# Block attention and a Fourier-mixing MLP on one core: the down product of the last batch in seven block products

## The chip, the cores and the metric

One core of a Trainium2 chip runs the whole program. The metric is device time in microseconds (us) for one execution. The engines are TensorE (PE; the loads of its stationary operand are shown as PEld), VectorE (DVE), ScalarE (ACT), GpSimd (POOL) and SyncE (SP), which issues most transfers.

## The reference

Inputs are q, k, v of shape 4 x 8 x 768 x 64 (batch, heads, positions, width) and two weight matrices, 512 x 2048 and 2048 x 512, all f32. Cut to what matters:

```python
# attention: each position sees its own block of 64 and the best 3 blocks by q . mean(k), causally
attn = softmax(where(mask, q @ k.T / 8, -1e9)) @ v
x    = attn as 4 x 768 x 512                      # heads side by side
u    = x + real(fft(fft(x, axis=1), axis=2))      # Fourier mixing
un   = (u - mean(u)) / sqrt(var(u) + 1e-6)        # over the last axis
out  = u + relu(un @ w_ch1) @ w_ch2               # the MLP: up, relu, down
```

## The kernel before, in words

The kernel works in stages that overlap. `attention(p)` treats a pair of heads, 16 pairs in all, four to a batch: casts (line 688) and small differences (461, 466) on POOL or DVE, transposes on TensorE (478, 527), block means and gates (497, 514, 542), the choice of three blocks on DVE (561 to 585), a POOL memset for a position's own block (594), the mask's transpose (606) and its spelling into extra rows of the query tile (616), scores (639), exponentials on ACT (650), the causal corners on POOL (656), and the product with v (668, `attend`), scaled on DVE (677, 680). `fourier(b)` mixes a batch: folds of x on DVE or POOL (700, 711, 721), two stages of products (739, 743; 773), the residual (779), statistics (786, 789), normalisation (813, 817) and a transpose into `unT` (831, 688).

`mlp(b)` works on a batch of 768 rows in two halves of 384. In a half the up product makes 16 tiles, each 128 hidden units by 384 rows, from four steps of 384 columns (line 853). Relu (865 on ACT, 867 on DVE) writes them as f16 into `hT[half]`. The down product makes three row tiles of 128 x 512, each from 16 steps of 512 columns over the hidden units (line 878); the stationary operand is a 128 x 128 piece of `hT`, the moving one a tile of `w2`. DVE adds the result to `U`, which holds u, in place (line 884), and SyncE writes the 128 x 512 tile out (256 KB; the call at 887, issued by the helper at 367).

No order is written by hand. `Plan.op` collects every operation with what it reads and writes, a rank, and an assumed duration for each engine that could do it. `Plan.schedule` then lays all operations out in time by those durations: on each engine it takes the operation that can start first, ties by rank, and where two engines could do a thing, it chooses the one that would end it earlier. The eight PSUM banks are handed out there as well, with a cap for each kind. The order found is what the engines execute. A POOL operation marked `port` waits for the DVE operation marked `port` ahead of it. Products of an earlier batch's MLP so fill TensorE while attention waits for other engines; the last batch's MLP, number 3, has nothing left beside it.

Of the kernel before, what the change touches and what calls it, by code (L numbers as in the profile page):

```python
# [12 lines left out]
FP = mybir.dt.float32  # L13
F16 = mybir.dt.float16
# [4 lines left out]
OP = mybir.AluOpType  # L19

S = 768
DM = 512
NB = 12
NST = 6
# [58 lines left out]
class Plan:  # L83
# [53 lines left out]
    def schedule(self):  # L137
        ops = self.ops
        free = dict(PE=1.0, ACT=1.5, DVE=0.9, POOL=0.9, SP=0.75)
        ready = {e: [] for e in free}  # L140
        for o in ops:
            o.wait = len(o.deps)
            o.ready = o.rel
            for d in o.deps:
                ops[d].users.append(o.i)
        cand = {e: set() for e in free}

        def offer(o):
# [12 lines left out]
        order = []  # L161
        left = len(ops)
        while left:
            best = None
            for e, c in cand.items():
                now = free[e]
                pick = None
                for i in c:
                    o = ops[i]
                    t = o.ready  # L170
                    blocked = False
                    for p in o.ps:
                        if p.bank is None:
                            if used[p.kind] >= self.CAPS[p.kind] or not banks:
                                blocked = True
                                break
                            t = max(t, banks[0][0])
                    if blocked:
                        continue
                    if o.port and e in ("DVE", "POOL"):  # L180
                        t = max(t, port_free + (self.LAT["DVE"] if e == "POOL" and holder else 0.0))
                    if o.dma and e != "POOL" and len(landing[e]) >= self.DEPTH:
                        t = max(t, landing[e][-self.DEPTH])
                    if len(o.engs) > 1:
# [36 lines left out]
            if o.dma:  # L221
                mine, other = ("POOL", "SP") if e == "POOL" else ("SP", "POOL")
                go = max(dma_free[mine], free[e])
                shared = max(0.0, dma_free[other] - go)
                dma_free[mine] = go + (2 * o.dma if 2 * o.dma <= shared else o.dma + shared / 2)
                o.done = dma_free[mine] + 1.9
                landing[e].append(o.done)
            order.append(o)
            left -= 1
            for p in o.ps:  # L230
                p.left -= 1
                if p.left == 0:
                    heapq.heappush(releases, (o.done, p.bank, p.kind))
            for u in o.users:
                v = ops[u]
                v.wait -= 1
                at = o.done
                if e in v.engs and len(v.engs) == 1 and not o.dma:
                    at = free[e] + self.OWN[e]
                elif o.dma:  # L240
                    at += self.LANDING if st > 8.0 else 0.0
                elif "PE" in v.engs and o.done > self.SLACK_FROM:
                    at += self.SLACK
                v.ready = max(v.ready, at)
# [29 lines left out]
PT_W = _w  # L274
# [4 lines left out]
def kernel(  # L279
# [9 lines left out]
    nc = tc.nc  # L289
    B, H, _, D = q.shape  # L290
# [30 lines left out]
    w2 = sb([128, NIT, DM], F16, "w2")  # L321
    eps = sb([128, 1], FP, "eps")

    NQ, NH, NG, NV, NPT = 2, 2, 2, 3, 2
    qn = many(NQ, [128, 2, NST, 64], FP, "qn")
    kn = many(NQ, [128, NST, 2, 64], FP, "kn")
    vn = many(2, [128, 2, NST, 64], FP, "vn")
    qhl = many(NH, [128, 2, NST, 128], F16, "qhl")
    k16 = many(NH, [128, NST, 128], F16, "k16")
    klo = many(1, [128, NST, 128], F16, "klo")  # L330
    QG = [many(NG, [128, S], F16, f"qg{e}") for e in range(2)]
    ki_all = sb([128, 2 * NG, S], F16, "ki")
    KI = [[ki_all[:, 2 * i + e, :] for i in range(NG)] for e in range(2)]
    V16 = many(NV, [128, 2, NST, 66], F16, "v16")
# [10 lines left out]
    pm = sb([128, 2, 6, 257], F16, "pm")  # L345
# [17 lines left out]
    P = Plan()  # L363


    def dma(rank, e, dst, src, w, us, r=(), issue=0.45, rel=0.0):
        P.op(rank, {e: issue if e != "POOL" else 0.65}, lambda x, n: eng[x].dma_start(dst, src),
             r=r, w=w, dma=us, rel=rel)
# [5 lines left out]
    def small(rank, e, cost, fn, r=(), w=(), ps=(), pre=(), port=False, rel=0.0):  # L374
        engs = e if isinstance(e, dict) else {e: cost}
        P.op(rank, engs, fn, r=r, w=w, ps=ps, pre=pre, port=port, rel=rel)
# [464 lines left out]
            P.readers.setdefault(("x", x3, 0), []).append(P.last_w[("unT", st)])  # L841


    def mlp(b):
        base = 100000 + 1000 * b
        U, u2 = ub[b % 2], b % 2
        for hf in range(2):
            for it in range(NIT):
                hp_ = P.psum("mm")
# [12 lines left out]
                def relu(x, n, hf=hf, it=it, hp_=hp_):  # L862
# [3 lines left out]
                    else:  # L866
# [85 lines left out]
```

## Time and profile before

| | us |
|---|---|
| median of 3 runs (lowest, highest) | 313.94 (313.51, 314.13) |
| the profiled execution | 313.72 |
| its span, first to last instruction | 311.5 |
| TensorE busy | 301.3 |
| VectorE busy | 195.3 |
| ScalarE busy | 189.1 |
| GpSimd busy | 130.3 |

The granted TensorE clock is 0.999 of full speed over the span. How to read the rows: in the page's engine rows each digit is the busy share of one of 40 equal slices, in tenths. A row of a group has line, engine, operation, output and inputs with their shapes, a count, then the busy time in us, the mean duration of one in ns, and the engine's idle time ahead of them with what ended it. A row in order of time begins with its start and its length in us; rows that follow each other are merged (x3). Durations of neighbours on an engine can overlap, since they are pipelined. A row of a stretch (two times joined by a colon) has the length, the busy time and count of PE, PEld, DVE, ACT and POOL, the granted clock, the busy share of the DMA engines and the GB/s that they moved.

### The profile page before, as it was taken

What the parts mean: (1) busy time and instruction counts of PE and PEld (TensorE: products, weight loads), DVE (VectorE), ACT (ScalarE), POOL (GpSimd) and SP (SyncE); (2) the same over time, 40 slices, a digit from 0 to 9 for tenths busy, and PEclk for the clock granted to TensorE, in tenths of its full rate; (3) what the DMA queues carried; (4) which work ended last, traced back from release to release, by engine and by line L of the source; (5) the groups of instructions that cost most, each with busy time, mean ns of one, the idle gap of its engine ahead of it and who ended that gap; (6) DMA issues with size and microseconds to landing.
All of it is one profiled execution on the core that took longest, in us unless ns stands there. A gap on an engine that the chain in (4) does not pass through costs nothing.

```text
span 311.5 us, 8060 instructions
## 1 busy us (share of the span) xinstructions
PE 301.3 (97%) x3097; PEld 198.5 (64%) x3097; DVE 195.3 (63%) x652; ACT 189.1 (61%) x418; POOL 130.3 (42%) x251
## 2 busy tenths in 40 slices
PE   7999999999999999999999999999999999999994
PEld 4767676766647776666666876757655865554641
DVE  4797989997655899755548797856425694002001
ACT  2579898779508788478644699708661671540710
POOL 4258897836546181748273453837025000000000
PEclk9999999999999999999999999999999999999999
DMA  8999999990066351009320760010001001101001
GB/s 218 257 241 238 246 232 217 228 189 22 0 153 176 81 121 32 36 37 237 78 61 34 187 154 1 36 36 35 2 36 67 2 1 67 37 0 67 36 34 67
DMA packets 82085, 31.12 MB, mean 100 GB/s; under 512 B 75272, under 2 KB 77492, under 8 KB 82048
## 3 DMA queue, kind: packets, MB, share of 16 engines
q1 hardware_dynamic: 77584, 25.77, 33.7%
q0 software_dynamic: 3536, 4.56, 8.1%
q8 instruction: 24, 0.39, 0.5%
q10 hardware_dynamic: 928, 0.30, 0.4%
q14 instruction: 13, 0.11, 0.1%
HBM read 28.52 MB, written 6.29 MB: 112 GB/s over the span
## 4 chain that ended last, share of the span: by engine, by line
PE 80%; DVE 9%; ACT 6%; issue 1%; DMA 1%; SPq 0%; DVEq 0%; ACTq 0%
PE bank L878 27%; PE bank L853 26%; PE bank L639 9%; PE bank L668 5%; ACT pt L650 4%; PE bank L527 3%; PE bank L739 2%; DVE u L779 2%; PE bank L773 2%; PE bank L478 2%; PE bank L831 1%; DMA kn<-in_k_dram 1%; DVE bst L786 1%; DVE qg L616 1%; PE bank L492 1%
## 5 line engine op out<-in xcount | busy, mean ns | idle before, releaser
L650 ACT ACTIVATE pt<-bank 128x512 f16<-128x512 f32 x192 | 88.3, 579 | 23.4 <-PE bank L639 21.7
L853 PE MATMUL bank<-unT,w 128*128 128x384 f16 x512 | 90.7, 326 | 0.2 <-DVE unT L688 0.2
L878 PE MATMUL bank<-w,hT 128*128 128x512 f16 x384 | 89.1, 379 | 0.0
L865 ACT ACTIVATE hT<-bank 128x384 f16<-128x384 f32 x115 | 56.3, 497 | 46.4 <-PE bank L853 45.6
L853 PEld LDWEIGHTS <-w 128*128 128x128 f16 x512 | 48.2, 98 | 30.0 <-issue 0.8
L878 PEld LDWEIGHTS <-hT 128*128 128x128 f16 x384 | 36.0, 98 | 37.6
L639 PE MATMUL bank<-qg,ki 76*128 76x128 f16 (+3 forms) x384 | 51.2, 259 | 0.7 <-ACT pt L650 0.4
L884 DVE TENSOR_TENSOR u<-bank,u 128x512 f32<-128x512 f32 x24 | 16.5, 688 | 51.1 <-PE bank L878 51.0
L639 PEld LDWEIGHTS <-ki 76*128 76x128 f16 x384 | 29.2, 97 | 10.6 <-issue 0.6
L656 POOL TENSOR_SCALAR_AFFINE_SELECT pt<-pt 128x512 f16<-128x512 f16 (+1 forms) x44 | 22.0, 522 | 25.3 <-ACT pt L650 20.6
L668 PEld LDWEIGHTS <-pt 128*128 128x128 f16 x672 | 23.8, 97 | 6.5 <-ACT pt L650 3.0
L668 PE MATMUL bank<-v,pt 128*128 128x65 f16 x672 | 25.6, 193 | 0.6 <-ACT pt L650 0.3
L616 DVE TENSOR_SCALAR qg<-bank 12x384 f16<-12x384 f16 x64 | 20.6, 322 | 7.6 <-PE bank L606 5.7
L466 POOL TENSOR_TENSOR klo<-kn,k 128x384 f16<-128x384 f32 x24 | 21.9, 913 | 5.3 <-DVE rcp L677 1.9
L461 POOL TENSOR_TENSOR qhl<-qn,qhl 128x320 f16<-128x320 f32 x26 | 20.6, 792 | 6.2 <-DVE qhl L688 4.8
L688 POOL CAST k<-kn 128x384 f16<-128x384 f32 x24 | 12.2, 507 | 19.2 <-DVE fs L721 9.0
L688 DVE COPY ki<-bank 64x768 f16<-64x768 f16 x23 | 12.7, 554 | 9.6 <-PE bank L478 7.0
L680 DVE TENSOR_TENSOR x<-bank,rcp 128x384 f16<-128x384 f32 x32 | 17.8, 555 | 0.6
L677 DVE RECIPROCAL rcp<-bank 128x6 f32<-128x6 f32 x32 | 6.2, 193 | 18.0 <-PE bank L668 10.6
L527 PE MATMUL bank<-sm,qhl 128*128 128x128 f16 x192 | 17.1, 229 | 0.1
L779 DVE TENSOR_TENSOR u<-bank,x 128x512 f32<-128x512 f32 x24 | 15.3, 681 | 1.9 <-PE bank L773 1.9
L594 POOL MEMSET gmp<- 64x5 f16 x40 | 4.6, 114 | 27.9 <-DVE gmp L585 26.8
(106 smaller groups left out, 405.6 us busy)
## 6 DMA issues: line engine op xcount, KB each, us to landing
out_dram<-u SPq DMA_DIRECT2D x24, 256.0 KB, 2.0
kn<-in_k_dram SPq DMA_DIRECT2D x28, 192.0 KB, 3.4
vn<-in_v_dram SPq DMA_DIRECT2D x28, 192.0 KB, 3.8
qn<-in_q_dram SPq DMA_DIRECT2D x26, 192.0 KB, 4.4
w<-in_moe_w_ch_dram POOLq DMA_DIRECT2D x16, 256.0 KB, 6.7
hT<-in_k_dram SPq DMA_DIRECT2D x4, 192.0 KB, 4.3
hT<-in_q_dram SPq DMA_DIRECT2D x4, 192.0 KB, 4.2
hT<-in_v_dram SPq DMA_DIRECT2D x4, 192.0 KB, 3.7
```

Source lines behind the costliest of these rows:

```text
L466: lambda x, n, kh=kh, kl=kl, e=e: eng[x].tensor_tensor(out=kl, in0=kn[a][:, :, e, :], in1=kh, op=OP.subtract),
L527: nc.tensor.transpose(bank16[tq.bank][:, 128 * st:128 * st + 128], qhl[h2][:, e, st, :], id16)
L616: nc.vector.tensor_scalar(out=rows[:, i::2, :], in0=turned[at:at + NB, 0:3 - i, :], scalar1=-NEG, scalar2=NEG, op0=OP.mult, op1=OP.add)
L639: nc.tensor.matmul(bank32[sp.bank][:, co:co + a1 - a0], KI[e][g3][0:76, 128 * jt:128 * jt + 128], QG[e][g3][0:76, a0:a1], start=not added, ...
L650: lambda x, n, sp=sp, pt=pt, at=at, wid=wid: nc.scalar.activation(out=pt[:, at:at + wid], in_=bank32[sp.bank][:, 0:wid], func=AF.Exp, scal ...
L656: lambda x, n, pt=pt, at=at, nd=nd: nc.gpsimd.affine_select(out=pt[:, at:at + 128 * nd].rearrange("p (a c) -> p a c", a=nd), in_=pt[:, at: ...
L668: nc.tensor.matmul(o[:, st, 0:65], pt[:, col:col + 128], V16[v4][:, e, jt, 0:65], start=(i == 0), stop=(i == 20))
L688: return eng[x].tensor_copy(out=dst, in_=src)
L779: lambda x, n, kt=kt, mp=mp: nc.vector.tensor_tensor(out=U[:, kt, :].rearrange("p (l r) -> p r l", r=2), in0=bank32[mp.bank].rearrange("p ...
L853: nc.tensor.matmul(bank32[hp_.bank][:, 0:384], w1[:, dt, 128 * it:128 * it + 128], unT[:, dt, 384 * hf:384 * hf + 384], start=(dt == 0), s ...
L865: nc.scalar.activation(out=o, in_=i_, func=AF.Relu)
L878: nc.tensor.matmul(bank32[cp.bank], hT[hf][:, it, 128 * j:128 * j + 128], w2[:, it, :], start=(it == 0), stop=(it == NIT - 1))
```

## The change

The last batch's down product is a 768 x 2048 by 2048 x 512 product. It is cut into 2 x 2 blocks on each side: rows into the two halves, hidden units into two times eight tiles, output columns into two times 256. Eight block products become seven by the scheme of Strassen: five sums of blocks on each side, seven products, and twelve additions or subtractions of their results into the four quarters of the output.

- `weight_sums` makes the five sums of quarters of `w2` on DVE, each in two instructions of 128 x 1024, into `WB`.
- `hidden_sums` makes the five sums of quarters of the hidden activations on DVE, tile by tile of 128 x 384, as soon as relu has written the tiles: 40 instructions, into `HA`.
- `down_seven` runs, for each of three pairs of row tiles, seven products of eight steps with 256 columns, and adds each into one or two quarters of `U` on DVE, 128 x 256 at a time. A quarter that is complete is written out at once (128 KB): twelve transfers.
- `WB` and `HA` need space. The buffers of attention are cut from four larger tiles (`loads_`, `turned_`, `keys_`, `vals_`), and `WB` and `HA` lie over parts of two of them; they wait for the last readers of what they cover.
- In the planner the test for a free bank is written for several new banks at once.

For the last batch both halves of the up product come first and the down product then. The other batches are computed as before.

```diff
--- Plan.schedule
-                    blocked = False
-                    for p in o.ps:
-                        if p.bank is None:
-                            if used[p.kind] >= self.CAPS[p.kind] or not banks:
-                                blocked = True
-                                break
-                            t = max(t, banks[0][0])
-                    if blocked:
-                        continue
+                    new = [p for p in o.ps if p.bank is None]
+                    if new:
+                        if len(banks) < len(new) or any(
+                                used[p.kind] + len(new) > self.CAPS[p.kind] for p in new):
+                            continue
+                        t = max(t, banks[len(new) - 1][0])
--- buffers
-    qn = many(NQ, [128, 2, NST, 64], FP, "qn")
-    kn = many(NQ, [128, NST, 2, 64], FP, "kn")
...
-    PT = [many(NPT, [128, PT_W], F16, f"pt{e}") for e in range(2)]
+    loads_ = sb([128, 11520], F16, "loads")
+    turned_ = sb([128, 16896], F16, "turned")
...
+    qn = [cut(loads_, 4608 * i, 1536, 2, NST, dtype=FP) for i in range(NQ)]
...
+    PT = [[cut(turned_, PT_W * (2 * i + e), PT_W) for i in range(NPT)] for e in range(2)]
...
+    WB = [cut(loads_, 2048 * i, 2048, 8) for i in range(5)]
+    HA = [cut(turned_, 3072 * i, 3072, 8) for i in range(5)]
--- new, before mlp
+    SUMS = [(0, 3, OP.add), (2, 3, OP.add), (0, 1, OP.add), (2, 0, OP.subtract),
+            (1, 3, OP.subtract)]
+    OTHER = [(0, 3, OP.add), (1, 3, OP.subtract), (2, 0, OP.subtract), (0, 1, OP.add),
+             (2, 3, OP.add)]
+    def combine(rank, name, at, dst, x0, x1, op, r, n, pre):
+        small(rank, {"DVE": 0.05 + 0.00059 * n, "POOL": 0.12 + 0.00195 * n}, 0,
+              lambda x, n_: eng[x].tensor_tensor(out=dst, in0=x0, in1=x1, op=op),
+              r=r, w=[(name,) + at], pre=pre, port=True)
+    def weight_sums(rank):
+        for i, (a0, a1, op) in enumerate(OTHER):
+            for c in range(2):
+                src = quarter(lambda kh, nh: w2[:, 8 * kh + 4 * c:8 * kh + 4 * c + 4,
+                                                256 * nh:256 * nh + 256])
+                combine(rank, "WB", (i, c), WB[i][:, 4 * c:4 * c + 4, :], src[a0], src[a1], op,
+                        [("w2", g) for g in range(8)], 1024, UNDER["WB"]())
+    GOES = {1: [(0, OP.add), (3, OP.add)], 2: [(2, OP.add), (3, OP.subtract)],
+            3: [(1, OP.add), (3, OP.add)], 4: [(2, OP.add), (0, OP.add)],
+            5: [(1, OP.add), (0, OP.subtract)], 6: [(3, OP.add)], 7: [(0, OP.add)]}
+    DONE = {3: 1, 4: 2, 7: 0, 6: 3}
+    def hidden_sums(rank, g):
+        for i, (a0, a1, op) in enumerate(SUMS):
+            src = quarter(lambda mh, kh: hT[mh][:, 8 * kh + g, :])
+            keys = quarter(lambda mh, kh: ("hT", mh, 8 * kh + g))
+            combine(rank, "HA", (i, g), HA[i][:, g, :], src[a0], src[a1], op,
+                    [keys[a0], keys[a1]], 384, UNDER["HA"]())
+    def down_seven(b):
+        for j in range(3):
+            cols = slice(128 * j, 128 * j + 128)
+            A = {3: hT[0][:, 0:8, cols], 4: hT[1][:, 8:16, cols]}
+            A.update({i: HA[z][:, :, cols] for i, z in IDX.items()})
+            Bm = {2: w2[:, 0:8, 0:256], 5: w2[:, 8:16, 256:512]}
+            Bm.update({i: WB[z] for i, z in JDX.items()})
...
+            for i in (5, 2, 1, 4, 3, 7, 6):
+                mp = P.psum("mm")
+                def prod(x, n, i=i, mp=mp, A=A, Bm=Bm):
+                    for z in range(8):
+                        nc.tensor.matmul(bank32[mp.bank][:, 0:256], A[i][:, z, :], Bm[i][:, z, :],
+                                         start=(z == 0), stop=(z == 7))
+                P.op(base + 150 + j, {"PE": 0.86}, prod, r=need[i], w=[mp], ps=[mp])
+                for q_, sign in GOES[i]:
+                    small(base - 200000, "DVE", 0.33,
+                          lambda x, n, mp=mp, q_=q_, sign=sign, part=part: nc.vector.tensor_tensor(
+                              out=part(q_), in0=part(q_), in1=bank32[mp.bank][:, 0:256], op=sign),
+                          r=[mp, key(q_)] + pre_u, w=[key(q_)], ps=[mp])
+                    if i in (3, 4, 7, 6) and q_ == DONE[i]:
+                        dma(base - 200000, "SP",
+                            out[b, 128 * row:128 * row + 128, 256 * half:256 * half + 256],
+                            part(q_), [("out", b, row, half)], 0.5, r=[key(q_)])
--- mlp
+        seven = b == B - 1
+        if seven:
+            weight_sums(102160)
...
+                if seven and hf and it >= 8:
+                    hidden_sums(base - 200000, it - 8)
+            if seven:
+                continue
...
+        if seven:
+            down_seven(b)
```

More of the change, by code (lines that the diff above doesn't have):

```diff
@@ L324, with cut @@
     NQ, NH, NG, NV, NPT = 2, 2, 2, 3, 2
-    qn = many(NQ, [128, 2, NST, 64], FP, "qn")
-    kn = many(NQ, [128, NST, 2, 64], FP, "kn")
[L327 to L332, printed above, removed]
+    loads_ = sb([128, 11520], F16, "loads")
+    turned_ = sb([128, 16896], F16, "turned")
+    keys_ = sb([128, 3072], F16, "keys")
+    vals_ = sb([128, 2376], F16, "vals")
+    def cut(t, at, n, *dims, dtype=F16):
+        v_ = t[:, at:at + n]
+        v_ = v_ if dtype == F16 else v_.bitcast(dtype)
+        names = "abc"[:len(dims)]
+        return v_ if not dims else v_.rearrange(
+            f"p ({' '.join(names)} z) -> p {' '.join(names)} z", **dict(zip(names, dims)))
+    qn = [cut(loads_, 4608 * i, 1536, 2, NST, dtype=FP) for i in range(NQ)]
+    kn = [cut(loads_, 4608 * i + 1536, 1536, NST, 2, dtype=FP) for i in range(NQ)]
+    vn = [cut(loads_, 4608 * i + 3072, 1536, 2, NST, dtype=FP) for i in range(2)]
+    klo = [cut(loads_, 9216, 768, NST)]
+    k16 = [cut(loads_, 9984 + 768 * i, 768, NST) for i in range(NH)]
+    qhl = [cut(turned_, 10752 + 1536 * i, 1536, 2, NST) for i in range(NH)]
+    QG = [[cut(turned_, 13824 + 1536 * i + 768 * e, 768) for i in range(NG)] for e in range(2)]
+    ki_all = cut(keys_, 0, 3072, 2 * NG)
     KI = [[ki_all[:, 2 * i + e, :] for i in range(NG)] for e in range(2)]
-    V16 = many(NV, [128, 2, NST, 66], F16, "v16")
+    V16 = [cut(vals_, 792 * i, 792, 2, NST) for i in range(NV)]
     GA = many(2, [128, 24], F16, "ka")
@@ L344 @@
     fs = sb([128, 2, 3, DM], F16, "fs")
-    pm = sb([128, 2, 6, 257], F16, "pm")
+    pmf = sb([128, 3084], F16, "pm")
+    pm = pmf.rearrange("p (r t d) -> p r t d", r=2, t=6)
     fk = fs.rearrange("p r t d -> p (r t) d").rearrange("p t (i d) -> p t i d", i=4)
@@ L841, in fourier, with below @@
             P.readers.setdefault(("x", x3, 0), []).append(P.last_w[("unT", st)])
+    def below(*names):
+        return [k_ for k_ in list(P.last_w) if isinstance(k_, tuple) and k_[0] in names]
+    UNDER = dict(
+        WB=lambda: below("qn", "kn", "vn", "klo", "k16"),
+        HA=lambda: below("pt", "qg", "qm", "qh", "ql", "qz"),
+    )
+    SUMS = [(0, 3, OP.add), (2, 3, OP.add), (0, 1, OP.add), (2, 0, OP.subtract),
+            (1, 3, OP.subtract)]
+    OTHER = [(0, 3, OP.add), (1, 3, OP.subtract), (2, 0, OP.subtract), (0, 1, OP.add),
+             (2, 3, OP.add)]
@@ new lines, in combine, with quarter @@
+    def combine(rank, name, at, dst, x0, x1, op, r, n, pre):
+        small(rank, {"DVE": 0.05 + 0.00059 * n, "POOL": 0.12 + 0.00195 * n}, 0,
+              lambda x, n_: eng[x].tensor_tensor(out=dst, in0=x0, in1=x1, op=op),
+              r=r, w=[(name,) + at], pre=pre, port=True)
+    def quarter(get):
+        return [get(0, 0), get(0, 1), get(1, 0), get(1, 1)]
+    def weight_sums(rank):
[5 more added lines that the diff above has]
+                        [("w2", g) for g in range(8)], 1024, UNDER["WB"]())
@@ new lines, in down_seven @@
+    def down_seven(b):
+        base = 100000 + 1000 * b
+        U, u2 = ub[b % 2], b % 2
+        for j in range(3):
[4 more added lines that the diff above has]
+            Bm.update({i: WB[z] for i, z in JDX.items()})
+            need = {i: ([("HA", IDX[i], g) for g in range(8)] if i in IDX else
+                        [("hT", int(i == 4), (8 if i == 4 else 0) + g) for g in range(8)])
+                    + ([("WB", JDX[i], z) for z in range(2)] if i in JDX else
+                       [("w2", (0 if i == 2 else 4) + z) for z in range(4)]) for i in range(1, 8)}
+            place = [(j, 0), (j, 1), (3 + j, 0), (3 + j, 1)]
+            part = lambda q_, place=place: U[:, place[q_][0], 256 * place[q_][1]:256 * place[q_][1] + 256]
+            key = lambda q_, place=place: ("u", u2, place[q_][0], place[q_][1])
+            pre_u = [("u", u2, st) for st in (j, 3 + j)]
+            for i in (5, 2, 1, 4, 3, 7, 6):
[6 more added lines that the diff above has]
+                for q_, sign in GOES[i]:
+                    row, half = place[q_]
+                    small(base - 200000, "DVE", 0.33,
[6 more added lines that the diff above has]
+                            part(q_), [("out", b, row, half)], 0.5, r=[key(q_)])
```

2 lines of the change are left out of this document (added).

## The prediction

> **What bounds the kernel now.** I read the page first, then the chain of work that ended last, then the rows of the stages that the change touches.
>
> ```profile
> span 311.5 us, 8060 instructions
> PE 301.3 (97%) x3097; PEld 198.5 (64%) x3097; DVE 195.3 (63%) x652; ACT 189.1 (61%) x418; POOL 130.3 (42%) x251
> ...
> PE   7999999999999999999999999999999999999994
> ...
> DVE  4797989997655899755548797856425694002001
> ...
> POOL 4258897836546181748273453837025000000000
> ```
>
> TensorE (PE) is busy for 97% of the span, in nearly every slice at 9, so what counts is TensorE's own time. VectorE (DVE) has room, most of all in the last quarter. GpSimd (POOL) has nothing from slice 32 on. The chain, in order of time (start, length, what):
>
> ```profile
> 247.03 2.62 PE bank L773 x24
> ...
> 261.80 4.10 PE bank L878 x19
> 265.90 10.40 PE bank L853 x64
> 276.31 10.36 PE bank L878 x48
> 286.67 10.40 PE bank L853 x64
> 297.06 10.37 PE bank L878 x48
> 307.44 0.04 DVEq L884
> 307.47 0.04 issue
> 307.52 0.69 DVE u L884
> ```
>
> From 265.90 to 307.43 only the last batch's MLP runs: up product (L853), down product (L878), each in two halves, gapless on TensorE, and then one addition (L884) and the output. The profiled execution took 313.72 us for its span of 311.5; the median of the runs is 313.94, 0.22 above it. I sum against 313.72 and add the 0.22.
>
> **TensorE in the down product.** Before: 96 steps of 512 columns in 10.36 + 10.37 = 20.73 us, 215.9 ns each. After: 7 products x 3 row pairs x 8 = 168 steps of 256 columns, each with its own weight load. Such steps stand in the trace: L773, 24 steps of 256 columns, a new weight load at each, 2.62 / 24 = 109.2 ns. 168 x 109.2 = 18.35 us. **Term 1: -2.38 us.**
>
> The row to doubt is the weight load, since there are 72 more of them:
>
> ```profile
> L878 PEld LDWEIGHTS <-hT 128*128 128x128 f16 x384 | 36.0, 98 | 37.6
> L668 PE MATMUL bank<-v,pt 128*128 128x65 f16 x672 | 25.6, 193 | 0.6 <-ACT pt L650 0.3
> ```
>
> A load is busy 98 ns, under 109.2; and L668, with a load at each step and only 65 columns, has 38 ns per step (25.6 / 672), so loads overlap each other and hide. The Trainium skill, "TensorE: Matmul & The Clock Gate", section "Back-to-back issue gap", speaks against the change: it gives a sustained stream of load and matmul 131 ns per step at 512 columns and about 81 at 128, which by a straight line between them is 98 ns at 256; by it 96 steps would be 12.6 us and 168 steps 16.4, a loss of 3.8 us. The trace does not bear the page out: 215.9 and 109.2 ns here.
>
> **VectorE's sums of hidden activations** (`hidden_sums`, 40 of 128x384, all f16 in SBUF). Rows by shape, and three neighbours in the order of time:
>
> ```profile
> L680 DVE TENSOR_TENSOR x<-bank,rcp 128x384 f16<-128x384 f32 x32 | 17.8, 555 | 0.6
> L884 DVE TENSOR_TENSOR u<-bank,u 128x512 f32<-128x512 f32 x24 | 16.5, 688 | 51.1 <-PE bank L878 51.0
> L700 DVE TENSOR_TENSOR fs<-x 128x384 f16<-128x384 f16 x25 | 8.0, 352 | 0.2
> ...
> 235.30 0.36 DVE L700 TENSOR_TENSOR fs<-x 128x384 f16<-128x384 f16 x1
> 235.57 0.68 DVE L884 TENSOR_TENSOR u<-bank,u 128x512 f32<-128x512 f32 x1
> ```
>
> The two rows with f32 input from PSUM give 1.04 ns per column and 0.155 us fixed. The f16 row of 384 takes 0.352, so 0.51 ns per column, and the next instruction starts 0.27 after it: unwaited instructions overlap by 0.08. In the changed kernel's instruction order, 16 of the 40 sums need activations of the first 24 tiles and lie under the second up product, where VectorE is idle (the zeros in its row). The last 24 come as triplets, one per tile of the last eight. When those tiles come:
>
> ```profile
> 295.80 0.49 ACT L865 ACTIVATE hT<-bank 128x384 f16<-128x384 f32 x1 [0.16 <-PE bank L853]
> 296.45 0.49 ACT L865 ACTIVATE hT<-bank 128x384 f16<-128x384 f32 x1 [0.16 <-PE bank L853]
> 297.10 0.49 ACT L865 ACTIVATE hT<-bank 128x384 f16<-128x384 f32 x1 [0.16 <-PE bank L853]
> ```
>
> One each 0.65 us, the last ending 0.53 after its product's stage (297.59 against 297.06). After the change the second up product follows the first at once: from 276.31 to 286.71. The ninth tile is ready at 286.71 + 0.53 - 7 x 0.65 = 282.69, and eight triplets of 3 x 0.27 = 0.81 end at 289.2 (not overlapping, at 0.352: 291.1). TensorE starts the products in the order 5, 3, 4, 6, 2, 1, 7 for the first row pair; 5, 3, 4 and 6 need nothing of the triplets. At 8 x 109.2 = 0.874 each it comes to product 2 at 290.21 and to its last step at 290.97. So the sums are in time by 1.8 us, and at the slower reading about level. Cost 0; the cover is those four products, and without it up to 0.2 us.
>
> **VectorE's additions into the result** (36 of 128x256 instead of 6 of 128x512, in `down_seven`). By the two f32 rows one is 0.155 + 256 x 0.00104 = 0.42 us, 0.34 overlapped. Twelve per row pair are 4.1 us beside 6.1 us of products. They queue behind the triplets: start 289.2, first row pair at product speed from 291 on. Eight banks hold the products meanwhile: the ninth, at 286.71 + 8 x 0.874 = 293.7, needs the bank of the first, which is added by 290. Cost 0. Their own reads after writes lie two or more instructions apart, which lets them overlap; if none overlapped, see the rivals. At the very end one addition of 256 columns stands where one of 512 stood: 0.69 to 0.42, **term 2: -0.27 us.**
>
> **The output in quarters.** 12 transfers of 128 KB for 6 of 256 KB: each still 128 rows, of 1 KB instead of 2.
>
> ```profile
> 308.24 0.33 SPq L367 DMA_DIRECT2D out_dram<-u  x1
> out_dram<-u SPq DMA_DIRECT2D x24, 256.0 KB, 2.0
> 301.00:304.50 3.50, 3.50 (x18) 1.61 (x17) 0.73 (x2) 0.00 (x0) 0.00 (x0) 1.00 0.20 75
> 308.00:311.50 3.50, 0.00 (x0) 0.00 (x0) 0.21 (x1) 0.00 (x0) 0.00 (x0) 0.88 0.20 75
> ```
>
> An issue takes SyncE 0.33 us and lands 2.0 later; the last four come 0.87 apart or a little less, so the queue keeps up. In a stretch of 3.5 us with one transfer the engines are busy for 0.20 x 3.5 = 0.70 us. Halving the bytes saves between 0 (fixed cost per piece) and 0.35 (all by bytes); nearer to bytes than to pieces is unknown, I take 0.25. **Term 3: -0.25 us.** The Trainium skill, "DMA: Bandwidth & Descriptors", section "Anatomy of one DMA", has 2.0 us fixed plus bytes at 436 GB/s (fitted to another queue kind), which would make it 0.30; the 2.0 us to landing here already contains the transfer.
>
> **VectorE's sums of weights** (`weight_sums`, 10 of 128x1024). By the f16 row: 0.155 + 1024 x 0.00051 = 0.68 us, 0.60 overlapped, 6 us in all, among the last pair's attention. The planner also moves work there: one up product ahead of L514 (`spread`), the second L668 (`attend`) behind the gates (L542) and three more up products, L606 (`m_turn`) behind four down steps.
>
> ```profile
> 216.97 0.20 PE L514 MATMUL bank<-ka,sm 128*128 128x24 f16 x2
> ...
> 218.97 0.80 PE L668 MATMUL bank<-v,pt 128*128 128x65 f16 x21
> 219.61 0.40 PE L542 MATMUL bank<-kg,qg 128*128 128x24 f16 x10
> ...
> 226.30 1.04 PE L639 MATMUL bank<-qg,ki 76*128 76x128 f16 x9
> ...
> 216.97 0.20 DVE L677 RECIPROCAL rcp<-bank 128x6 f32<-128x6 f32 x1 [0.84 <-ACT pt L650]
> 217.20 0.56 DVE L680 TENSOR_TENSOR x<-bank,rcp 128x384 f16<-128x384 f32 x1
> ...
> 221.50 0.81 DVE L581 MAX8 mx<-gsb 128x8 f32<-128x12 f32 x10
> 222.42 0.28 DVE L585 TENSOR_TENSOR gmp<-gsb,mx 128x120 f16<-128x120 f32 x1
> 224.85 1.36 DVE L616 TENSOR_SCALAR qg<-bank 12x384 f16<-12x384 f16 x4 [2.15 <-PE bank L606]
> ...
> 222.76 0.57 POOL L594 MEMSET gmp<- 64x5 f16 x4 [5.21 <-DVE gmp L585]
> ```
>
> On TensorE, laid end to end from 216.97: ten up products at 0.65 (10.40 / 16), L668 0.64 (219.61 - 218.97), sixteen down steps 3.45, the small L514, L542 and L606 together an estimated 0.5: the last pair's scores (L639) are reached at 228.1 instead of 226.30, with no gap and the same work in all. On VectorE, ten sums and the queue between them (two reciprocals at 0.20, two L680 at 0.56, MAX8 0.81, L585 0.28, two L700 at 0.27, the other gate steps about 0.2 each, and the wait for the gates until 220.1) let L616 start at 225.7 and end at 227.1: 1 us ahead of the scores. The 0.57 on POOL ends at 223.5, ahead of L606 at 225.3. POOL's masks of the pair before now wait for a weight sum each (an added wait, up to 1.5 us later); what needs them, the second L668, has moved from 218.97 to about 221.8. If the 1 us is gone, TensorE stalls by what is over. Cost 0. The fourier step's reversed sums (L711) move from POOL to VectorE, which is 3.08 us there to about 1 here, so its start does not slip.
>
> Everything earlier (buffers cut from four larger tiles, the planner's test for several banks at once) leaves the order and the kinds of waits as they are: 0, but a gain or a loss of 0.1 cannot be excluded.
>
> **Sum:** -2.38 - 0.27 - 0.25 = -2.90; 313.72 - 2.90 = 310.82, and against the median 311.04.
>
> **Rivals.**
> A, slower: VectorE takes the f16 sums at the f32 rate (the L680 row, 0.475 overlapped for 384 columns). Against it stand 25 executions of L700 at 0.352. A price in the same trace that leans its way is this:
>
> ```profile
> 239.33 1.30 DVE L711 TENSOR_TENSOR pm<-fs 128x1530 f16<-128x1530 f16 x1
> 236.73 3.08 POOL L711 TENSOR_TENSOR pm<-fs 128x1530 f16<-128x1530 f16 x1
> ```
>
> 1530 columns should take 0.94 and took 1.30 beside a POOL instruction. POOL is idle under the hidden sums. At the f32 rate the triplets end at 282.69 + 8 x 1.43 = 294.1 and product 2 waits about 3 us; ten weight sums at 1.22 make L616 late by 5.4, a stall of about 4. Time: 311.0 + 7 = 318; it decides from about 0.42 us per hidden sum and 0.95 per weight sum on.
> B, a small gain: VectorE bounds the end, its additions never overlapping (0.42 plus 0.04 between dependent ones, 36 x 0.46 = 16.5 us) behind triplets that end at 291.1: last addition at 307.6 instead of 305.6, 313.0.
> C: the spells come late, POOL beside the weight sums stretching them by the 1.30 / 0.94 seen above: ten sums 2.5 us longer, a stall of 1.5: 312.5.
> D, slower: weight loads do not hide at 256 columns in a stream of 168. L773 shows only 24 in a row. 72 more loads at 98 ns are 7.1 us: 318; from 41 ns per load on it is a loss.
>
> **How the numbers follow.** Forecast 0.74 (310.4 to 311.7), B 0.08, C 0.05 (both a gain or level), A 0.06, D 0.02, slower in a way not seen here 0.05. Change within 0.2% (0.6 us, about what a measurement of this kernel can tell from none) gets 0.04, from the edge of B and from partial A; slower 0.12; faster 0.84. The range takes in the bounds of terms 2 and 3 below and B above: 310.3 to 313.1, with 0.13 left out, nearly all above.
>
> **What would show it.** Right: TensorE without a gap from 210 to the end; the 168 steps in 18.3 us; L616 done before the scores; hidden sums at 0.35; the last addition 0.42. Wrong: idle TensorE ahead of L639 at 228 (C, A), ahead of product 2 (A), the additions still running 1 us after the last product (B), steps over 120 ns (D).

## The result, and the profile after

| | median, us | lowest to highest | executions |
|---|---|---|---|
| before | 314.09 | 313.51 to 317.55 | 11 |
| changed | 312.49 | 310.78 to 313.93 | 11 |

The ratio is 0.9938, with an interval of 0.9913 to 0.9963: faster, by less than 1%, and by 1.6 us and not by the 2.9 of the sum. The median lies inside the wide range of 310.3 to 313.1, but outside the forecast's own 310.4 to 311.7, at a place that the prediction had given to rivals C and B (312.5 and 313.0). So most of this part asks where 1.3 us went. The profiled execution took 312.49 us. The changed kernel's page:

```profile
span 310.3 us, 8310 instructions
...
PE 296.3 (95%) x3169; PEld 203.8 (66%) x3169; DVE 224.2 (72%) x733; ACT 189.9 (61%) x419; POOL 127.2 (41%) x249
...
PE   6899996899999999999999999999999999999994
...
DVE  3897988798746889856547898866955695147884
...
PEclk9799999999999999999999999999999999999999
```

TensorE is busy for 5.0 us less (301.3 before), VectorE for 28.9 more (195.3). TensorE's 5.0 us are twice what the products save: 3.6 of them are missing in the first 60 us already (51.25 busy, 54.84 before), where the change takes no work out. VectorE's new work is seen at the end of its row (147884 where 002001 stood), and TensorE's row shows none of it: it is at 9 from slice 8 on. But in slices 6 and 7 it is at 6 and 8, and before it was at 9 there: a hole at 47 to 62 us, far from the change. The chain of work that ended last, in order of time (start, length, what):

```profile
262.06 5.18 PE bank L976 x24
267.24 20.80 PE bank L947 x128
288.04 18.35 PE bank L921 x168
306.42 0.42 DVE u L927
```

The last batch's MLP is now one up product of 128 steps (L947, before L853), the seven products (L921) and one addition (L927). It lasts from 267.24 to 306.84, 39.60 us; before it went from 265.90 to 308.21, 42.31. That is -2.71. But it began 1.34 us later. A single profile of each thus says that 1.3 us were lost ahead of the last part, and the experiments test whether the change lost them.

The covers that the forecast named, in order of time in the changed kernel (L628 was L616, L651 was L639, L870 the sums):

```profile
227.19 1.36 DVE L628 TENSOR_SCALAR turned<-bank 12x384 f16<-12x384 f16 x4
...
229.37 1.04 PE L651 MATMUL bank<-turned,keys 76*128 76x128 f16 x9
...
290.24 0.35 DVE L870 TENSOR_TENSOR turned<-hT,hT 128x384 f16<-128x384 f16 x1
...
291.37 0.82 PE L921 MATMUL bank<-w,turned 128*128 128x256 f16 x6
```

The spells end at 228.55, 0.8 us ahead of the scores; the last hidden sum ends at 290.59, 0.8 ahead of product 2's start.

### The profile page after: what moved, and what is told of

Its sections match the earlier page's. It is cut to its first block, busy times and chain, and to the rows that moved or that the text cites. A ratio compares the mean times of both kernels' runs of the same rounds, so it can differ in the third digit from the quotient of the medians.

```text
span 310.3 us, 8310 instructions
## 1 busy us (share of the span) xinstructions
PE 296.3 (95%) x3169; PEld 203.8 (66%) x3169; DVE 224.2 (72%) x733; ACT 189.9 (61%) x419; POOL 127.2 (41%) x249
## 3 DMA queue, kind: packets, MB, share of 16 engines
q0 software_dynamic: 3536, 4.56, 8.2%
## 4 chain that ended last, share of the span: by engine, by line
PE 75%; DVE 9%; DMA 5%; ACT 4%; POOL 3%; issue 3%; SPq 0%; POOLq 0%
PE bank L947 26%; PE bank L976 20%; PE bank L651 7%; PE bank L921 6%; DMA loads<-in_q_dram 5%; PE bank L680 4%; PE bank L539 3%; ACT turned L662 2%; PE bank L751 2%; DVE u L791 2%; PE bank L785 2%; PE bank L843 1%; DVE turned L628 1%; POOL turned L473 1%; PE bank L490 1%
## 5 line engine op out<-in xcount | busy, mean ns | idle before, releaser
L662 ACT ACTIVATE turned<-bank 128x512 f16<-128x512 f32 x192 | 88.4, 579 | 25.1 <-PE bank L651 23.4
L947 PE MATMUL bank<-unT,w 128*128 128x384 f16 x512 | 90.8, 326 | 0.2 <-DVE unT L700 0.2
L976 PE MATMUL bank<-w,hT 128*128 128x512 f16 x288 | 68.1, 379 | 0.0
L947 PEld LDWEIGHTS <-w 128*128 128x128 f16 x512 | 48.1, 97 | 29.6 <-issue 0.8
L651 PE MATMUL bank<-turned,keys 76*128 76x128 f16 (+3 forms) x384 | 51.1, 259 | 0.7 <-ACT turned L662 0.4
L651 PEld LDWEIGHTS <-keys 76*128 76x128 f16 x384 | 29.2, 97 | 10.6 <-issue 0.6
L668 POOL TENSOR_SCALAR_AFFINE_SELECT turned<-turned 128x512 f16<-128x512 f16 (+1 forms) x44 | 22.1, 522 | 29.6 <-ACT turned L662 20.4
L680 PEld LDWEIGHTS <-turned 128*128 128x128 f16 x672 | 23.9, 97 | 6.0 <-ACT turned L662 2.2
L680 PE MATMUL bank<-vals,turned 128*128 128x65 f16 x672 | 25.6, 193 | 0.2
L628 DVE TENSOR_SCALAR turned<-bank 12x384 f16<-12x384 f16 x64 | 20.6, 321 | 5.5 <-PE bank L618 3.6
L478 POOL TENSOR_TENSOR loads<-loads 128x384 f16<-128x384 f32 x24 | 22.0, 915 | 3.4 <-DVE x L829 1.6
L473 POOL TENSOR_TENSOR turned<-loads,turned 128x320 f16<-128x320 f32 x26 | 21.3, 819 | 5.0 <-DVE turned L700 3.6
L539 PEld LDWEIGHTS <-turned 128*128 128x128 f16 x192 | 12.8, 101 | 6.1 <-POOL turned L473 3.7
```

The costliest lines, as they stand in the source:

```text
L473: lambda x, n, hi=hi, lo=lo, e=e: eng[x].tensor_tensor(out=lo, in0=qn[a][:, e, 1:NST], in1=hi[:, 1:NST], op=OP.subtract),
L478: lambda x, n, kh=kh, kl=kl, e=e: eng[x].tensor_tensor(out=kl, in0=kn[a][:, :, e, :], in1=kh, op=OP.subtract),
L539: nc.tensor.transpose(bank16[tq.bank][:, 128 * st:128 * st + 128], qhl[h2][:, e, st, :], id16)
L628: nc.vector.tensor_scalar(out=rows[:, i::2, :], in0=turned[at:at + NB, 0:3 - i, :], scalar1=-NEG, scalar2=NEG, op0=OP.mult, op1=OP.add)
L651: nc.tensor.matmul(bank32[sp.bank][:, co:co + a1 - a0], KI[e][g3][0:76, 128 * jt:128 * jt + 128], QG[e][g3][0:76, a0:a1], start=not added, ...
L662: lambda x, n, sp=sp, pt=pt, at=at, wid=wid: nc.scalar.activation(out=pt[:, at:at + wid], in_=bank32[sp.bank][:, 0:wid], func=AF.Exp, scal ...
```

## The experiments

Two explanations stood against each other for the missing 1.3 us. Theory 1: the changed kernel costs time in the early part, by its buffers, its planner or the transfers there. Theory 2: nothing is lost, but executions of either kernel differ in their first 60 us by more than that, and one profile and eleven times of each did not sort this out. (The expectations of e1 and e2 have the two names the other way round: what they call theory 1 is theory 2 here. Those of e9 and e11 have them as here.)

**e1: the buffers and the planner's test, without the seven products.**

```diff
-        seven = b == B - 1
+        seven = False
```

> The new buffers and the planner's new test, with the old down product for the last batch as well. Theory 1 (the 1.3 us that the changed kernel's profile has lost before its last stages come from when the loads of 30 to 60 us happen to land, in executions of either kernel): same as before, ratio 0.999 to 1.001, single times spread like those of before. Theory 2 (cutting the buffers from larger tiles costs time in the early part): slower than before by about 1.3 us, ratio near 1.004, and the late part of the profile as before.

Median 314.58 us (313.57 to 317.25), ratio 1.0014, interval 0.9982 to 1.0046. Its stretch of 40 to 60 us (stretch; its length; busy time and count of PE, PEld, DVE, ACT, POOL; granted clock; DMA share; GB/s) has no hole:

```profile
40.00:60.00 20.00, 18.75 (x309) 14.45 (x307) 17.89 (x65) 16.89 (x41) 16.58 (x27) 1.00 1.20 224
```

By itself the interval would still allow a loss of 1.4 us. The executions at a granted clock of 0.997 or more are narrower: seven of e1 have a median of 313.96 us, 43 of the kernel before one of 314.02. So the buffers and the planner cost nothing that these runs can tell from none.

**e2: the changed kernel under another name.** No edit.

> The changed kernel unchanged, on the same chip as the others. Both theories: ratio 0.991 to 0.996. From the start of the last batch's up product to the last addition 39.6 us (20.80 + 18.35 + 0.45), whatever the total. Theory 1: the start of that up product lies anywhere from 265 to 268 us and another profile need not show POOL waiting 3.8 us for loads of q at 44 to 49 us. Theory 2: it does show them.

Median 312.31 (311.04 to 313.29), ratio 0.9923, interval 0.9891 to 0.9956. In its profile, of 311.04 us, the last up product starts at 265.82, 1.4 us earlier than in the first profile of the same instructions and level with before. From there to the last addition it takes 39.60 us again, as expected. So the late start is not fixed to the kernel.

**e3: whole rows out, six transfers as before.**

```diff
-                    if i in (3, 4, 7, 6) and q_ == DONE[i]:
-                        dma(base - 200000, "SP",
-                            out[b, 128 * row:128 * row + 128, 256 * half:256 * half + 256],
-                            part(q_), [("out", b, row, half)], 0.5, r=[key(q_)])
+                if i in (7, 6):
+                    row = place[DONE[i]][0]
+                    dma(base - 200000, "SP", out[b, 128 * row:128 * row + 128, :], U[:, row, :],
+                        [("out", b, row)], 0.8, r=[("u", u2, row, 0), ("u", u2, row, 1)])
```

> The changed kernel with its last output in six transfers of 128x512 instead of twelve of 128x256. The prediction took 0.25 us for the quarters (bounds 0 and 0.35): 0.2 to 0.35 us slower than the changed kernel, and 2.0 us to landing for the last transfer instead of 1.7. If the quarters cost something (more issues and more pieces), this one is faster.

Median 312.25 (310.04 to 313.41), ratio 0.9918, interval 0.9886 to 0.9951: level with the changed kernel, and not 0.2 to 0.35 us slower. The traces tell the two apart where the times don't. From the end of the last addition to the end of the span, whole rows take 3.25 us here (307.43 + 0.42 to 311.1) and 3.29 in the kernel before (308.21 to 311.5). Quarters take 3.46 in the first profile (306.84 to 310.3) and 3.48 in e2. All 13 profiles, those of the runs below included, fall into these two groups: 3.25 to 3.30 in the six with whole rows, 3.42 to 3.49 in the seven with quarters. The quarter itself does land sooner, 1.7 us after its issue instead of 2.0. What is longer stands behind it. SyncE's closing waits (first and last start), before and then changed, with the transfers of the changed kernel's last 32 us:

```profile
L947 SPq EVENT_SEMAPHORE  x11: 17/28/28, 308.6 to 311.4; - x11
L947 SPq DRAIN  x3: 7/7/7, 310.6 to 310.9; - x3
```

```profile
L1047 SPq EVENT_SEMAPHORE  x11: 17/28/28, 307.2 to 310.2; - x11
L1047 SPq DRAIN  x3: 7/7/7, 309.4 to 309.7; - x3
```

```profile
out_dram<-u SPq DMA_DIRECT2D x12, 128.0 KB, 1.7
```

SyncE waits for the queues one after the other; the first of its three drains comes 2.4 us after the last addition before (308.21 to 310.6) and 2.6 after it with quarters (306.84 to 309.4). Nine of the eleven closing waits stand ahead of that drain. In the order of time the trace has eight of these nine behind the last landing with quarters, and six before. They start 0.06 to 0.08 us apart, but for one step of 0.37 to 0.39 us, which all seven profiles with quarters have there and none of the six with whole rows. So the two more waits are the smaller part of what is longer, and the one long step the larger; what SyncE does in it the profile does not show.

**e4: no weight sums.** The products take quarters of `w2` in place of their sums, so that the last batch's output is not the reference's.

```diff
-        if seven:
-            weight_sums(102160)
...
-            Bm.update({i: WB[z] for i, z in JDX.items()})
+            Bm.update({i: w2[:, 8 * (z % 2):8 * (z % 2) + 8, 256 * (z // 2 % 2):256 * (z // 2 % 2) + 256] for i, z in JDX.items()})
```

> The changed kernel without the ten sums of weights: the products take quarters of the weights themselves, so that part of the computation is left out. The prediction put the sums at 0, hidden under TensorE's work: same time as the changed kernel within 0.3 us, TensorE without a gap from 200 us on in both. Rival C (they make the masks late): up to 1.5 us faster, with the gap ahead of the last pair's scores gone.

Median 311.98 (310.52 to 316.24), ratio 0.9919, interval 0.9882 to 0.9956. Seven microseconds less work on VectorE and no time gained that could be told from none: the weight sums are hidden.

**e5 and e6: the transfers of the MLP's weights 8 us later**, in the kernel before and in the changed one. The same edit in both:

```diff
-                weight(28.0 + 2.0 * i, w1[:, dt, 1024 * hf:1024 * hf + 1024],
+                weight(36.0 + 2.0 * i, w1[:, dt, 1024 * hf:1024 * hf + 1024],
...
-                weight(44.0 + 2.0 * g, w2[:, 2 * g:2 * g + 2, :],
+                weight(52.0 + 2.0 * g, w2[:, 2 * g:2 * g + 2, :],
```

> The kernel before, with the 16 transfers of the MLP's weights (issued by GpSimd between its other work) planned 8 us later. Theory 1a (the loads of q, k and v between 30 and 60 us share full DMA engines with the weights, so that how far ahead GpSimd happens to be decides whether it then waits for q): the waits of POOL for loads go, single times lie closer together than the 312.8 to 316.9 seen, median 0.3 to 1 us lower. Theory 1b (the loads alone fill the engines): no change of the spread.

> The changed kernel with the same later weights. Theory 1a: as in the kernel before, spread smaller than 310.8 to 313.9 and median 0.5 to 1.5 us lower; against the kernel before with late weights the gain is 2.5 us (-2.38 - 0.27 of the prediction, and the tail). Theory 1b: median and spread stay at 312.4 and 3 us.

e5: 316.85 (315.42 to 318.73) beside 314.67 for before, ratio 1.0063, interval 1.0034 to 1.0093, slower. e6: 314.07 (313.02 to 316.51), ratio 0.9984, interval 0.9952 to 1.0016. Both expectations had theory 1a gain time; both kernels lost some 2 us. That the weights only stand in the loads' way at 44 to 60 us, and do better later, falls. Two stretches of e5, and then the second one of before:

```profile
40.00:60.00 20.00, 19.10 (x311) 15.37 (x309) 18.33 (x64) 14.76 (x36) 14.66 (x24) 1.00 1.12 207
60.00:80.00 20.00, 17.94 (x211) 12.12 (x210) 17.47 (x57) 16.13 (x37) 9.82 (x21) 1.00 0.75 131
```

```profile
60.00:80.00 20.00, 19.77 (x237) 14.07 (x236) 17.94 (x58) 16.27 (x39) 11.01 (x23) 1.00 0.57 109
```

TensorE is fuller until 60 us (18.74 before) and loses 1.8 us in the next 20. The pair says something else as well: with the same later weights in both, the seven products gain 316.85 - 314.07 = 2.78 us by the medians, where 2.5 was expected. Part of that is the draw of executions: those at a clock of 0.997 or more alone have medians of 316.88 (8 of e5) and 314.77 (5 of e6), 2.1 apart.

**e7: each hidden sum executed twice; e8: each weight sum executed twice.** To see how near the covers are to their ends. e7 (in e8 the name is `WB`):

```diff
-              lambda x, n_: eng[x].tensor_tensor(out=dst, in0=x0, in1=x1, op=op),
+              lambda x, n_: [eng[x].tensor_tensor(out=dst, in0=x0, in1=x1, op=op)
+                             for _ in range(2 if name == "HA" else 1)][-1],
```

> Each of the 40 sums of hidden activations is executed twice, in the same order of instructions. The prediction has them hidden up to about 0.42 us each and TensorE waiting ahead of product 2 from there on. Twice is 0.36 + 0.03 + 0.27 = 0.66 us, so the triplets end about 9 us later and the products about 7 us (6 to 8): the span of the last part, from the start of the last up product, 46.5 us instead of 39.6. If the sums had more cover than stated, less.

> Each of the 10 sums of weights is executed twice, in the same order. The prediction has a cover of 1 us ahead of the last pair's scores. Ten more at about 0.70 make the mask rows 7 us later and leave TensorE idle for about 6 us (5 to 7) between 225 and 235 us, and the whole 6 us longer; with no such wait, VectorE has room there that the prediction did not see.

e7 took 324.66 us, e8 318.30, one execution of each. In e7 the steps of product 2 wait for the triplets, just where rival A put its wait (two of four such waits, then the stretch of the products):

```profile
296.06 0.28 PE L922 MATMUL bank<-w,turned 128*128 128x256 f16 x1 [1.67 <-DVE turned L870]
...
298.05 0.28 PE L922 MATMUL bank<-w,turned 128*128 128x256 f16 x1 [1.70 <-DVE turned L870]
```

```profile
290.50:318.90 28.40, 21.30 (x168) 17.12 (x166) 24.68 (x73) 0.49 (x1) 0.00 (x0) 0.88 0.14 48
```

The four waits (1.67, 1.70, 1.70, 1.59) are 6.7 us, as expected. On top, the same 168 steps took 21.30 us of TensorE instead of 18.35, while the granted clock fell to 0.88 in this stretch. So the last part took 49.26 us (269.66 to 318.92) and not the 46.5 expected: 3 us more than the waits' own length. In e8 the waits of TensorE from 215 to 240 us (in the changed kernel it has none from 200 on) are:

```profile
PE bank L680 <- POOL turned L668: 1.8, 1, 1.8
PE bank L651 <- DVE turned L628: 1.7, 1, 1.7
PE bank L618 <- POOL gmp L606: 1.1, 1, 1.1
```

4.6 us for 6.9 us of added sums (5 to 7 were expected), at the three places where the forecast looked for them: masks, spells and the gates' transpose. So both covers are real and small; the sums are not free for any longer duration.

**e9: the kernel before under another name, and e11: the changed kernel once more, on the same chip.** No edits. Theory 2 needs the kernel before to show the hole, too.

> The kernel before under another name: ratio 1.000 by every theory. What is asked is how far two sets of some ten executions of one kernel lie apart, and which granted clocks and which times they show. Theory 2 (the part up to 60 us differs from execution to execution in both kernels): executions at a clock of 1.0 at 313.6 to 314.5 and one or more at 0.99 or below, 1 to 3 us away, as in the changed kernel. Rival 2a (the changed kernel brings the differences with it): this one stays within 0.3 us.

> The changed kernel under another name, on the same chip as the copy of the kernel before. Theory 2: executions whose clock is the same in both kernels lie 2.3 to 2.8 us apart, whatever the medians do (expected medians 311.2 to 312.5). Rival 2a (1 us or more was lost for good in the early part by the changed kernel): no more than 1.8 us apart at the same clock.

e9: median 315.72 us (313.41 to 318.19), ratio 1.0019, interval 0.9979 to 1.0059 against the same instructions at 314.09. Medians of a dozen executions of one kernel lie 1.6 us apart, as much as the first measurement of the change. e11: 311.32 (310.26 to 314.26), ratio 0.9906, interval 0.9870 to 0.9942.

The profile of e9 has the hole. Three stretches in the profile before, in the first profile of the changed kernel, and in e9:

```profile
7.60:11.00 3.40, 3.35 (x25) 2.44 (x26) 2.09 (x8) 1.38 (x3) 0.79 (x1) 1.00 1.29 264
...
40.00:60.00 20.00, 18.74 (x308) 14.44 (x305) 17.90 (x64) 16.89 (x42) 16.55 (x26) 1.00 1.19 223
```

```profile
7.60:11.00 3.40, 3.10 (x26) 2.41 (x25) 3.07 (x9) 1.38 (x3) 1.60 (x3) 0.50 1.25 270
...
40.00:60.00 20.00, 16.34 (x271) 12.80 (x268) 16.62 (x59) 14.41 (x36) 14.88 (x23) 1.00 1.20 231
```

```profile
7.60:11.00 3.40, 3.19 (x26) 2.58 (x27) 2.90 (x9) 1.51 (x3) 1.77 (x3) 0.53 1.25 266
...
40.00:60.00 20.00, 16.28 (x271) 12.80 (x268) 15.51 (x59) 14.15 (x35) 14.14 (x23) 1.00 1.06 196
```

The second and the third are alike, and they are different kernels: TensorE at half clock from 7.6 to 11 us, and 16.3 us of work in the 20 where the first has 18.7. In this hole GpSimd waits for the loads of q and k (all of it in 30 to 60 us), in the changed kernel and in e9; the profile before has no such wait there:

```profile
POOL turned L700 <- DMA loads<-in_q_dram: 3.8, 2, 2.5
```

```profile
POOL k L688 <- DMA kn<-in_k_dram: 3.2, 2, 2.3
POOL qhl L688 <- DMA qn<-in_q_dram: 1.3, 1, 1.3
```

Why these loads come late is not shown: the DMA share is above 1 in all three over the 20 us, but in e9 it is 0.79 at 48 to 52 us, inside the hole. With equal starts the two kernels can be compared piece by piece. The end of the chain in e9:

```profile
267.52 10.40 PE bank L853 x64
...
309.13 0.69 DVE u L884
```

The last part starts at 267.52 there and at 267.24 in the changed kernel; it lasts 42.30 us to the end of the addition, against 39.60; the whole execution took 315.38 us, against 312.49.

The executions with a granted clock on record can be sorted by it: before is what ran beside the experiments and e9, changed is the first measurement, e2 and e11 (medians in us):

| granted clock | before | changed | difference |
|---|---|---|---|
| 0.997 to 1.0 | 314.02 (43) | 311.58 (10) | -2.44 |
| 0.991 to 0.995 | 313.44 (21) | 310.95 (10) | -2.49 |
| 0.984 to 0.989 | 316.37 (26) | 313.28 (10) | -3.09 |
| all | 314.23 (90) | 311.80 (30) | -2.43 |

The first row is the clean one: its ten executions of the changed kernel (311.18 to 312.26) all lie under its 43 of the kernel before (313.58 to 315.95). The second row is not of one kind. In the changed kernel it has seven executions at 0.994 with a median of 310.78 and three at 0.995 with one of 312.59; at 0.995 alone the two kernels are 0.82 us apart, with three executions on one side. So the clock sorts the executions only in part, and the 2.4 us rest on the first row.

There theory 2 holds: at a clock of 0.997 or more the change gains 2.4 us, and nothing of 1 us or more is lost for good. The profiles alone would not have settled it, since the hole (262 to 284 matmuls in 40 to 60 us, instead of 308 or 309) is in all seven of the changed kernel and its variants with the weights in the same place (the first, e2, e3, e4, e7, e8 and e11), and in one of three without the seven products (e9, not before and e1). Nor do the counts say that the change brings it: the first row has 10 of 30 executions of the changed kernel and 43 of 90 of the one before, the last 10 of 30 and 26 of 90, which are no differences that these numbers could show. The first eleven executions of the changed kernel had four of the last row; their median was unlucky by 0.7 us.

**e10: whole rows, and the weights 8 us earlier.** A try at a faster version, on top of e3:

```diff
-                weight(28.0 + 2.0 * i, w1[:, dt, 1024 * hf:1024 * hf + 1024],
+                weight(20.0 + 2.0 * i, w1[:, dt, 1024 * hf:1024 * hf + 1024],
...
-                weight(44.0 + 2.0 * g, w2[:, 2 * g:2 * g + 2, :],
+                weight(36.0 + 2.0 * g, w2[:, 2 * g:2 * g + 2, :],
```

> The seven products with the output in whole rows, and the weights' transfers released 8 us earlier (20 and 36 instead of 28 and 44 in the planner's time), since 8 us later was slower. If the place of the weights among the loads of q, k and v is worth as much in the other direction, 1.5 to 2.5 us under the changed kernel, about 310. If the later weights were slower only because they end later, no change: 311.5 to 312.5. If earlier weights take the DMA engines from the attention's loads, slower: 313 to 315.

Median 317.98 us (315.79 to 322.78), ratio 1.0096, interval 1.0050 to 1.0142: slower than before. Its chain has one long wait for a load of k, and a stretch at two thirds of the clock follows:

```profile
31.73 10.50 DMA hT<-in_k_dram
```

```profile
40.00:60.00 20.00, 17.16 (x221) 12.68 (x218) 11.57 (x52) 13.41 (x30) 12.83 (x20) 0.67 1.17 241
```

This fits that earlier weights take the DMA engines from the attention's loads, though the time is 3 us beyond the 313 to 315 expected of it; later ones cost TensorE at 60 to 80 us. Of the three places tried, the one in both kernels is the best. No version tried beats the changed kernel by anything that can be measured.

## Why the prediction was right, and where it was not

- **Term 1, -2.38: right.** 168 steps took 18.35 us in all three of the changed kernel's profiles, 109.2 ns each, as L773's 24 steps had promised. Rival D is out: 168 loads hide as 24 do.
- **Term 2, -0.27: right.** The last addition took 0.42 us. Terms 1 and 2 give -2.65; the last part became 2.71 shorter (the rest is the gap ahead of the addition, 0.09 before and 0.03 now).
- **The sums at nothing: right, with slightly less to spare than counted.** The rows by shape of the changed kernel:

```profile
L927 DVE TENSOR_TENSOR u<-u,bank 128x256 f32<-128x256 f32 x36 | 13.1, 415 | 3.2 <-PE bank L921 2.2
...
L870 DVE TENSOR_TENSOR turned<-hT,hT 128x384 f16<-128x384 f16 x24 | 7.9, 351 | 2.6 <-ACT hT L959 2.6
L870 DVE TENSOR_TENSOR loads<-w 128x1024 f16<-128x1024 f16 x10 | 6.9, 702 | 0.1
```

  Hidden sums at 351 ns (0.352 forecast) and additions at 415 (0.42) rule out A and B; weight sums at 702 (0.68), beside POOL too, rule out C. The spells were 0.8 us ahead of the scores instead of 1.0, and the hidden sums 0.8 ahead of product 2's start as worked out from 289.2 and 290.21 (1.0). e7 and e8 show these margins by using them up, and show the waits at the places named. The added wait of POOL's masks came, too, 4.6 us in all, and nothing waited for the masks:

```profile
L668 POOL TENSOR_SCALAR_AFFINE_SELECT turned<-turned 128x512 f16<-128x512 f16 x22 | 14.0, 636 | 28.0 <-ACT turned L662 20.4 <-DVE loads L870 3.3 <-DVE nmr L817 2.9
...
L668 POOL TENSOR_SCALAR_AFFINE_SELECT turned<-turned 128x256 f16<-128x256 f16 x22 | 9.0, 408 | 1.6 <-DVE loads L870 1.3 <-ACT hT L959 0.3
```

- **Term 3, -0.25: wrong in sign.** This is the step that failed. The landing did shorten by 0.3 us, but the forecast took it for the end of the span. The end of the span is SyncE's closing waits, and from the last addition to there quarters took 0.17 us more (3.46 against 3.29); e3 with whole rows has the old figure back. With +0.17 the sum is -2.48, and the table above has -2.44 in its first row and -2.43 over all.
- **Everything earlier at 0, give or take 0.1: right for the change, wrong as a statement on a measurement.** e1 and the first row of the table show no loss there. But the forecast took one profile, at a clock of 0.999, as the kernel's time, where executions of the same instructions lie from 312.5 to 318.2. The measured gain of 1.6 us instead of 2.9 is two things: 0.4 from term 3, and the rest from which executions were drawn (0.7 in the changed kernel, 312.49 for 311.80 over all; 0.1 in the one before, 314.09 for 314.23).
- **The range: met with luck.** The first median stands at rival C's time, but C's waits are not in the trace: TensorE waits for nothing from 200 us on. It fell into the range by the room left for rivals that did not come. The executions of the table's first row, with a median of 311.58, bear the forecast's own 310.4 to 311.7 out; those of the last row, with one of 313.28, lie outside the whole range.

What decides an execution's start is open: no run changed it by intent.

## What to carry to other kernels

Before a gap between forecast and median is explained from two profiles, look whether the difference lies where the change is: here the change's own stage came out to 0.06 us, and the gap lay 200 us ahead of it. A copy of the old kernel, measured like the new one, with its executions sorted by granted clock, settled what edits of the new kernel could not. And a smaller last transfer need not end a kernel sooner: here it landed 0.3 us sooner and the span ended 0.17 later. Count the time from the last computation to the end of the span, not to the landing.

## What was not expected of the hardware

- **The clock at the start.** TensorE's granted clock fell to 0.50 to 0.66 between 7.6 and 11 us in ten of the 13 profiles, e9 and e5 (with the kernel before) among them, and stayed at 1.00 there in three: before, e1 and e7. Where it fell, TensorE had been quicker ahead of it, with 19 to 22 instructions between 4 and 7.4 us against 11 or 12. This stretch, before and then changed:

```profile
4.00:7.40 3.40, 2.75 (x12) 1.92 (x10) 1.33 (x4) 0.96 (x2) 1.58 (x3) 1.00 1.22 320
```

```profile
4.00:7.40 3.40, 2.20 (x20) 1.62 (x18) 1.11 (x3) 1.02 (x3) 1.58 (x3) 1.00 1.19 311
```

  The granted clock is 1.00 in both, and yet the same twelve f32 steps (L492, then L504) took 2.69 us before and 1.47 in the changed kernel: the granted clock in the records is not all that sets TensorE's pace early on.

```profile
5.51 2.69 PE L492 MATMUL bank<-ind,kn 128*128 128x2 f32 x12 [0.65 <-DMA kn<-in_k_dram]
```

```profile
5.81 1.47 PE L504 MATMUL bank<-ind,loads 128*128 128x2 f32 x12 [1.20 <-DMA loads<-in_k_dram]
```

  This fall does not decide the late start of the last part. In e2 the clock fell (0.63) and the last up product began at 265.82; in e7 it did not, and the last up product began at 269.66, though what e7 changes comes only after that.
- **Waits that cost more than their length.** After idle TensorE in e7 and e10 the granted clock fell (0.88 and 0.67 over the stretches shown). In e7 this added 3 us to 6.7 us of waits. That the idle time brought it about fits both, but was not tested by itself, and idle time alone does not always do it: in the first profile of the changed kernel TensorE was busy for only 4.56 us between 48 and 56 us, and its clock stayed at 1.00 there and until 64 us.
